# Talking-heads attention and a sparse-activation feed-forward on one core: a weight conversion two slots later, operand splits in other steps, two gates in another form

## The chip, the cores and the metric

The kernel runs on one core of a Trainium2 chip. The metric is the device time of one execution in microseconds (us); the median of three executions of the kernel before is 889.9 us (888.41 to 891.25).

The engines are called as in the profile: PE is TensorE's matmul and PEld its weight load, DVE is VectorE, ACT is ScalarE, POOL is GpSimd, and SP is the engine whose queue issues nearly all DMAs here. Each engine works through its own instructions in the order in which the program gives them and waits at an instruction until its semaphores allow it.

## What is computed

The reference, cut to what matters (batch 4, 12 heads, 448 rows, head size 64; then 1792 tokens, 768 wide, 2048 inner):

```python
scores = scale * np.matmul(q, k.transpose(0, 1, 3, 2))
scores = np.einsum('bhij,hg->bgij', scores, w_pre)
attn = np.exp(scores - scores.max(-1, keepdims=True))
attn = attn / (attn.sum(-1, keepdims=True) + 1e-9)
attn = np.einsum('bhij,hg->bgij', attn, w_post)
x = (attn @ v).transpose(0, 2, 1, 3).reshape(B * S, H * D)
h = x @ w_in
g = np.where(h >= 1, h, np.where(h <= -1, 0.0, (h + 1) ** 2 / 4))
out = g @ w_out
```

The two weights of the second half, w_in and w_out, come as float64, and the kernel turns them into float32 by integer work on their words.

## The kernel before

**Attention stage (to about 460 us).** The 16 tiles of 120 or 88 query rows are cut into blocks of ten rows times twelve heads; three groups of three or four blocks make a tile, so there are 48 groups, and the main loop (`for n in range(NG + 2)`) runs one group a turn, 8 to 11 us each. In a turn, every engine's order is: `load_s` of the next group (SP), `pre` (PE, the first head mix), `row_max` (DVE, L205), one `split` (DVE, L189 and L190), `exps` (ACT, L211), `norm` (DVE L217 and L218, then POOL L222), further splits, a first call of `convs`, `post` of the group before (PE L232, evicted by ACT L234), transposes, `pv` (PE L249), `scores` (PE L157, evicted by ACT L162 and DVE L166), late loads, and a second call of `convs`. One `post` of the group before stands among the exponentials. `pre`, `post`, `pv` and the scores share six PSUM buffers (`ps_l`), which `exps` and the evictions give back.

**The conversion.** `conv_units` has 64 chunks of 128 x 384 float64 values. Each goes through a load (SP L327, into `wraw`, three buffers), `scaled` (ACT L288), `lowest` (ACT L294), `shifted` (DVE L297), `sign` (DVE L303, the last reader of `wraw`), `add` (POOL L307) and a store (SP L334). The work is dealt out in slots: chunk n is loaded in slot 3n, and each later step follows at the lag that the table `lags` gives it. `convs(goal)` runs slots until their number reaches a goal; the goals are `share * (n - NC + 0.4)` in the middle of a group and `share * (n - NC + 1)` at its end, with `share` = slots / 41. There are 203 slots before. So most groups run two slots in the middle and three at the end, and which chunk's steps fall into which of the five places goes round every three groups. As 203 / 41 is 4.95, the pattern slips by one slot at group 22.

**First feed-forward product (about 461 to 679 us).** It is a seven-product scheme, in 56 steps `j`: `q, k = divmod(j, 7)`, with the first 28 steps over 2 x 512 tokens (phase 0) and the other 28 over 2 x 384 (phase 1). `step(j)` is 18 matmuls at L510 with the operand `xop[ph, k]` (named a0 to a6 and b0 to b6 in the profile). After it, a turn gives ACT and DVE in this order: `split_w(j + 2)` (ACT L399, DVE L402), `take_maxima` (DVE L555), a gate, `split_xb` (three times ACT L457 and DVE L458: one operand of phase 1), and `evict_f(j)`. `evict_f` is two copies on ACT (L570) for k = 0, 2 and 3, an addition on DVE (L572) for k = 1, 4 and 5. The products of k = 0, 2, 4 and 6 share one bank, so `step` of k = 6 has to wait for the eviction of k = 4. A `gate` in the short form is one ACT instruction (L538) and two on DVE (L549 and L550); in the long form it is three on ACT (L538, L545, L546) and one on DVE a step later (L555). After `split_xb(k)`, `load_xb` on SP fetches the pieces of the operand four places on.

**Second product (679 us to the end).** PE at L675 works without a break.

Of the kernel before, what the change touches and what calls it, by code (L numbers as in the profile page):

```python
# [22 lines left out]
def tile_talking_heads_moe(  # L23
# [248 lines left out]
    def convert(st, p):  # L272

        def halves():  # L280
            w = st["raw"].bitcast(I32).rearrange("p (n t) -> p n t", t=2)
            return w[:, :, 0], w[:, :, 1]

        def scaled():
            lo, hi = halves()
            if "t" not in st:
                st["t"] = p.tile([128, CW], I32, tag="wt", name="wt", bufs=4)
            nc.scalar.activation(out=st["t"].bitcast(F32), in_=hi.bitcast(F32), func=AF.Copy,  # L288
                                 scale=2.0 ** -111)

        def lowest():
            lo, hi = halves()
            st["k"] = p.tile([128, CW], I32, tag="wk", name="wk", bufs=2)
            nc.scalar.activation(out=st["k"], in_=lo.bitcast(U32), func=AF.Copy, scale=2.0 ** -29)  # L294

        def shifted():
            nc.vector.tensor_single_scalar(out=st["t"], in_=st["t"], scalar=3,  # L297
                                           op=ALU.logical_shift_left)

        def sign():  # L300
            lo, hi = halves()
            t = st["t"]
            nc.vector.scalar_tensor_tensor(out=t, in0=hi, scalar=-0x80000000, in1=t,  # L303
                                           op0=ALU.bitwise_and, op1=ALU.bitwise_or)

        def add():
            nc.gpsimd.tensor_tensor(out=st["t"], in0=st["t"], in1=st.pop("k"), op=ALU.add)  # L307

        return [scaled, lowest, shifted, sign, add]

    def conv_units():
        chunks = []
        for f in range(NF):
            for c in range(2):
                chunks.append((w_in[c * CW:(c + 1) * CW, f * 128:(f + 1) * 128]
                               .rearrange("(k p) f -> p k f", p=128), wsd[f, c]))
            for c in range(2):
                chunks.append((w_out[f * 128:(f + 1) * 128, c * CW:(c + 1) * CW],
                               wod[f, :, c * CW:(c + 1) * CW]))
        st = {}  # L320
        us = []

        def load(n):
            raw = qp.tile([128, CW], I64, tag="wraw", name="wraw", bufs=3)
            src = chunks[n][0]
            dst = raw if len(src.shape) == 2 else raw.rearrange("p (k f) -> p k f", f=128)
            nc.sync.dma_start(out=dst, in_=src)  # L327
            st[n] = {"raw": raw}
            st[n]["steps"] = convert(st[n], qp)

        def store(n):
            dst = chunks[n][1]
            src = st.pop(n)["t"].bitcast(F32)
            nc.sync.dma_start(out=dst, in_=src)  # L334


        lags = ((store, 11), (4, 6), (2, 4), (3, 4), (1, 3), (0, 2), (load, 0))
        for slot in range(3 * len(chunks) + 11):
            def unit(slot=slot):
                for f, lag in lags:  # L340
                    n, rest = divmod(slot - lag, 3)
                    if rest == 0 and 0 <= n < len(chunks):
                        if callable(f):
                            f(n)
                        else:
                            st[n]["steps"][f]()
            us.append(unit)
        return us
# [6 lines left out]
    NQ = NF // 4  # L355
# [71 lines left out]
    def split_w(j):  # L427
        if j < NJ:
            wts[j] = split_to(raw[KIND[j % 7], j // 7] if j < NJA else raw.pop(j))
# [22 lines left out]
    def split_x(x, r, k, ph):  # L452
        p, off = HOMES[ph][k]
        n = NH[ph]
        hi, lo = xop[ph, k, r] = [view(f"{'ab'[ph]}{k}{'hl'[i]}", p, off + 8 * n * r + 4 * n * i, n, dt=F32R)
                                     for i in range(2)]
        nc.scalar.activation(out=hi, in_=x, func=AF.Copy)  # L457
        nc.vector.tensor_tensor(out=lo, in0=x, in1=hi.bitcast(F32), op=ALU.subtract)  # L458
# [13 lines left out]
    def x_last(r):  # L472
        sum_x("B21", "B21", "B22", r)
# [18 lines left out]
    def load_xb(p):  # L492
        if p < 21:
            k, r = divmod(p, 3)
            piece[p] = view("xr", *RING[p % 12], NH[1])
            nc.sync.dma_start(out=piece[p], in_=x_src(XK[k], r, 1) if k in (0, 1, 5) else xtd[XK[k], r])

    def split_xb(k):
        for r in range(3):
            split_x(piece.pop(3 * k + r), r, k, 1)  # L500
        for r in range(3):
            load_xb(3 * k + r + 12)
# [22 lines left out]
    def slot(q, i, h):  # L525
        ph = q // NQ
        return gq[ph, q % NQ].rearrange("p (n i) t -> p n i t", i=2)[:, :, i, h * NH[ph]:(h + 1) * NH[ph]]
# [29 lines left out]
    def gate_slot(q, i, h, act=False):  # L557
        d = slot(q, i, h)
        gate(bk.pop(q) if (i, h) == (1, 0) else d, d, act)
# [161 lines left out]
    with tc.manual_schedule():  # L721
# [194 lines left out]
        for z in range(NQ):  # L916
            gq[0, z] = view("gq", "gg", 16384 * z, 4, NA)
            gq[1, z] = view("gq", *GHOME[z], 4, 2 * NH[1])
        XAT = {23: 0, 24: 1, 25: 2, 26: 3, 27: 4, 29: 5, 30: 6}
        for j in range(NJ):  # L920
            q, k = divmod(j, 7)
            ph = j // NJA
            end = q == NQ - 1
            if j:
                step(j)
                split_w(j + 2)
                take_maxima()
            else:
                evict_f(0)
            if k == 0 and q:  # L930
                gate_slot(q - 1, 1, 0)
            elif k == 1 and q:
                if ph == 0:
                    sum_w("A21", "A22", "A11", ALU.subtract, q)
                gate_slot(q - 1, 0, 1)
            elif k == 3:
                gate_slot(q, 0, 0, q > 0)
            elif k == 4 and q:
                gate_slot(q - 1, 1, 1, True)
            if j == 0:  # L940
                sum_w("S1", "A21", "A22", ALU.add, 0)
                sx("B12", 2, 4)()
                sx("B11", 2, 3)()
                x_last(2)
                for r, s in enumerate(("s4", "s2", "s6")):
                    load_xa("B22", r, s)
            elif j == 1:
                sum_w("A21", "A22", "A11", ALU.subtract, q)
            elif j == 2:
                for r in range(3):  # L950
                    split_xa("B22", r, 5)
            elif j == 3:
                for r in range(3):
                    split_xa("B21", r, 6)
            if ph == 0:
                if k == 0:
                    keep_w(2, q)
                    keep_w(3, q)
                elif k == 2:
                    sum_w("A12", "A12", "A11", ALU.subtract, q)  # L960
                    keep_w(4, q)
                    load_b(NJA) if end else load_a("A11", q + 1)
                elif k == 3:
                    keep_w(5, q)
                    load_b(NJA + 1) if end else load_a("A21", q + 1)
                elif k == 4:
                    if end:
                        load_b(NJA + 2)
                        load_b(NJA + 3)
                    else:  # L970
                        load_a("A22", q + 1)
                        load_a("A12", q + 1)
                elif k == 5 and not end:
                    sum_w("S1", "A21", "A22", ALU.add, q + 1)
                elif k == 6 and not end:
                    sum_w("A11", "S1", "A11", ALU.subtract, q + 1)
            load_b(j + 6) if j + 2 >= NJA else None
            if 4 <= j < 7:
                tx_load(j - 4)
            if 6 <= j < 18:  # L980
                tx_sum(j - 6)
            if 7 <= j < 19:
                tx_keep(j - 7)
            if 19 <= j < 22:
                for p in range(4):
                    load_xb(4 * (j - 19) + p)
            if j in XAT:
                split_xb(XAT[j])
            if j:
                evict_f(j)  # L990
            f = j - NJ + 3
            if f == 0:
                load_t(0)
                load_t(1)
            elif f == 1:
                split_t(0)
                load_t(2)
                prep_s(0)
            elif f == 2:
                split_t(1)  # L1000
                load_t(3)
                prep_s(1)
# [62 lines left out]
```

## Time and profile before

| | us |
|---|---|
| three executions: median (lowest to highest) | 889.9 (888.41 to 891.25) |
| the profiled execution: its time | 888.03 |
| the profiled execution: span from first to last instruction | 886.3 |
| PE busy in the span | 867.8 (98%) |
| DVE busy | 680.0 (77%) |
| ACT busy | 566.8 (64%) |
| POOL busy | 178.2 (20%) |

A busy PE in this profile is one with a matmul under way by its modelled end; the end is later than the moment from which the next matmul could be issued. Lines such as "L303" are lines of the kernel before; "SPq" is the instruction by which SP issues a DMA.

### The profile page before, as it was taken

The page shows a single profiled execution, that of the slowest core. Times are in us where ns is not written, and L with a number is a line of the kernel's source. Part 1 is how long each engine was busy: PE and PEld are TensorE (multiplying, and loading weights), DVE is VectorE, ACT ScalarE, POOL GpSimd, SP SyncE. Part 2 cuts the span into 40 slices and gives each one's busy share as a digit, 9 for nine tenths or more (in the row PEclk, how much of TensorE's full clock was granted, in tenths as well). Part 3 has the DMA queues.
Part 4 walks back from the last instruction along what each step waited for, and adds up shares of the span by engine and source line. Part 5 has one row for each costly group of instructions (what it writes and reads, how often), then busy time and mean ns, then how long its engine had stood idle before and what let it go on. Part 6 is the DMA issues. An engine that isn't in the chain of part 4 may idle for free.

```text
span 886.3 us, 17512 instructions
## 1 busy us (share of the span) xinstructions
PE 867.8 (98%) x6410; PEld 763.0 (86%) x6410; DVE 680.0 (77%) x1121; ACT 566.8 (64%) x1157; POOL 178.2 (20%) x253
## 2 busy tenths in 40 slices
PE   8999999999999999999999999999999999999998
PEld 6788888888888878878788788879999999999998
DVE  4887787888687887887568977788667987777853
ACT  4787677776877777877675566677667535433431
POOL 0334433543443533534220000000000000000000
PEclk9999999999999999999999999999999999999999
DMA  8768867888678887786355745654444453124341
GB/s 159 236 185 240 256 200 225 268 236 244 192 238 257 236 253 201 237 258 201 123 183 172 267 153 177 215 173 129 125 126 161 137 184 134 54 65 132 98 134 62
DMA packets 155832, 162.30 MB, mean 183 GB/s; under 512 B 64100, under 2 KB 149476, under 8 KB 155748
## 3 DMA queue, kind: packets, MB, share of 16 engines
q1 hardware_dynamic: 152964, 160.51, 59.6%
q10 hardware_dynamic: 2784, 0.69, 0.5%
q8 instruction: 51, 0.84, 0.4%
q14 instruction: 33, 0.27, 0.1%
HBM read 88.81 MB, written 33.82 MB: 138 GB/s over the span
## 4 chain that ended last, share of the span: by engine, by line
PE 82%; DMA 9%; ACT 4%; DVE 2%; SPq 2%; issue 1%; POOL 0%; ACTq 0%; DVEq 0%
PE ps_f L675 23%; PE ps_f L510 22%; PE ps_a L232 12%; PE ps_x L249 7%; PE ps_l L202 6%; PE ps_s L157 6%; PE ps_l L200 4%; DMA wraw<-in_moe_w_in_dram 3%; DMA s<-ssb 3%; DMA wraw<-in_moe_w_out_dram 2%; ACT e L211 1%; SPq L181 1%; PE ps_t L140 1%; ACT wt L288 1%; DMA qraw<-in_q_dram 1%
## 5 line engine op out<-in xcount | busy, mean ns | idle before, releaser
L222 POOL TENSOR_SCALAR wr<-wpost,rs 120x120 f32<-120x120 f32 x180 | 114.0, 649 | 264.1 <-DVE rs L218 212.7
L232 PEld LDWEIGHTS ps_a<-wr,e 120*112 120x112 f32 x1440 | 155.0, 177 | 12.8 <-issue 10.7
L232 PE MATMUL ps_a<-wr,e 120*112 120x120 f32 (+1 forms) x1440 | 157.0, 266 | 4.9 <-ACT e L211 4.9
L211 ACT ACTIVATE e<-ps_l,nm 120x448 f32<-120x448 f32 x180 | 112.5, 632 | 43.6 <-DVE nm L205 43.3
L658 ACT ACTIVATE sgh_p<-gq_p 128x1024 fp32r<-128x1024 f32 (+1 forms) x56 | 53.3, 953 | 90.8 <-PE ps_f L675 90.6
L205 DVE TENSOR_REDUCE nm<-ps_l 120x1 f32<-120x448 f32 x180 | 100.9, 615 | 6.1 <-PE ps_l L202 5.5
L402 DVE SCALAR_TENSOR_TENSOR wl<-wi,wh 128x768 fp32r<-128x768 f32 x71 | 67.6, 954 | 43.9 <-ACT wh L399 43.9
L675 PE MATMUL ps_f<-wh,sgl_p 128*128 128x384 f32 x294 | 98.2, 334 | 0.0
L675 PE MATMUL ps_f<-wh,sgh_p 128*128 128x384 f32 x294 | 98.2, 334 | 0.0
L675 PE MATMUL ps_f<-wl,sgh_p 128*128 128x384 f32 x294 | 98.2, 334 | 0.0
L234 ACT ACTIVATE aT<-ps_a 112x480 f32<-112x480 f32 x180 | 94.9, 597 | 3.4 <-PE ps_a L232 3.3
L399 ACT ACTIVATE wh<-wi 128x768 fp32r<-128x768 f32 x71 | 59.6, 842 | 58.2 <-PE ps_f L510 17.9
L202 PE MATMUL ps_l<-s,wpre 120*120 120x448 f32 x196 | 94.1, 563 | 0.2 <-DMA s<-ssb 0.2
L659 DVE TENSOR_TENSOR sgl_p<-gq_p,sgh_p 128x1024 fp32r<-128x1024 f32 (+1 forms) x56 | 60.9, 1088 | 35.8 <-ACT sgh_p L658 35.8
L249 PE MATMUL ps_x<-aT,v 112*64 112x120 f32 (+1 forms) x1536 | 83.5, 262 | 1.5 <-ACT aT L234 1.4
L249 PEld LDWEIGHTS ps_x<-aT,v 112*64 112x64 f32 x1536 | 73.8, 137 | 7.6 <-ACT aT L234 2.7
L166 DVE COPY ssb<-ps_s 120x448 f32<-120x448 f32 (+1 forms) x96 | 57.3, 619 | 17.2 <-PE ps_s L157 17.1
L307 POOL TENSOR_TENSOR wt<-wt,wk 128x384 int32<-128x384 int32 x64 | 64.2, 1010 | 20.6 <-ACT wk L294 15.2
L162 ACT ACTIVATE ssb<-ps_s 120x448 f32<-120x448 f32 (+1 forms) x96 | 51.9, 548 | 17.3 <-PE ps_s L157 14.3
L200 PE MATMUL ps_l<-sh,wpre_h 120*120 120x448 f32 (+1 forms) x82 | 58.6, 715 | 0.0
L190 DVE TENSOR_TENSOR sl<-s,sh 120x448 fp32r<-120x448 f32 (+1 forms) x82 | 54.2, 662 | 2.8
L675 PEld LDWEIGHTS ps_f<-wh,sgh_p 128*128 128x128 f32 x294 | 55.2, 188 | 0.0
(210 smaller groups left out, 1837.0 us busy)
## 6 DMA issues: line engine op xcount, KB each, us to landing
s<-ssb SPq DMA_DIRECT2D x172, 210.0 KB
wraw<-in_moe_w_in_dram SPq DMA_DIRECT2D x32, 384.0 KB
wraw<-in_moe_w_out_dram SPq DMA_DIRECT2D x32, 384.0 KB
wi<-wod SPq DMA_DIRECT2D x29, 384.0 KB
wi<-wsd SPq DMA_DIRECT2D x28, 384.0 KB
wsd<-wt SPq DMA_DIRECT2D x32, 192.0 KB
wod<-wt SPq DMA_DIRECT2D x32, 192.0 KB
wi<-wss SPq DMA_DIRECT2D x16, 384.0 KB
```

The lines of the kernel that those rows point to most:

```text
L200: nc.tensor.matmul(out=lps[m], lhsT=w[:k], rhs=y[:k], start=(j == 0), stop=(j == 2))
L202: nc.tensor.matmul(out=lps[m], lhsT=wpre[:k], rhs=x[:k], start=True, stop=True)
L205: nc.vector.tensor_reduce(out=nm, in_=lps[m], axis=AX.X, op=ALU.max, negate=True)
L211: nc.scalar.activation(out=e, in_=ps, func=AF.Exp, bias=nm, accum_out=sm[:, j:j + 1])
L222: nc.gpsimd.tensor_scalar_mul(out=w[:, :, :ni], in0=wpost[:, :, :ni], scalar1=rs[:, j:j + 1])
L232: nc.tensor.matmul(out=ps[:, r, :ni * H], lhsT=e[:, r * KP:(r + 1) * KP], rhs=w[:, :, :ni], start=True, stop=True)
L234: nc.scalar.activation(out=aT[t][:, :, :, c:c + ni], in_=ps[:, :, :ni * H].rearrange("q r (h i) -> q r h i", h=H), func=AF.Copy)
L249: nc.tensor.matmul(out=ps[s * D:(s + 1) * D, m, :n], lhsT=vt[b, g][:, 2 * m + s, r * D:(r + 1) * D], rhs=a[:, r, 4 * g + 2 * m + s, :n], s ...
L307: nc.gpsimd.tensor_tensor(out=st["t"], in0=st["t"], in1=st.pop("k"), op=ALU.add)
L402: nc.vector.scalar_tensor_tensor(out=lo, in0=t, scalar=2.0 ** -8, in1=hi.bitcast(F32), op0=ALU.mult, op1=ALU.subtract)
L510: nc.tensor.matmul(out=o, lhsT=u[:, c, k], rhs=x, start=first and r == 0 and m == 0, stop=r == 2 and m == 2, skip_group_check=True)
L675: nc.tensor.matmul(out=o, lhsT=x[:, f, c], rhs=y[:, f % 2, :], start=first and f == 0 and m == 0, stop=hf == 1 and f == 3 and m == 2, skip ...
```

## The change

All steps of a conversion but its load come two slots later (their distances to one another stay), which makes 205 slots out of 203. The phase 1 operands are split in the steps 23, 23, 26, 27, 27, 30 and 31 in place of 23, 24, 25, 26, 27, 29 and 30. The gates at k = 3 of q = 3 and q = 4 (steps 24 and 31) take the short form, as the one of q = 0 does.

```diff
-        lags = ((store, 11), (4, 6), (2, 4), (3, 4), (1, 3), (0, 2), (load, 0))
-        for slot in range(3 * len(chunks) + 11):
+        lags = ((store, 13), (4, 8), (2, 6), (3, 6), (1, 5), (0, 4), (load, 0))
+        for slot in range(3 * len(chunks) + 13):
...
-        XAT = {23: 0, 24: 1, 25: 2, 26: 3, 27: 4, 29: 5, 30: 6}
+        XAT = {23: (0, 1), 26: (2,), 27: (3, 4), 30: (5,), 31: (6,)}
...
             elif k == 3:
-                gate_slot(q, 0, 0, q > 0)
+                gate_slot(q, 0, 0, q not in (0, NQ - 1, NQ))
...
-            if j in XAT:
-                split_xb(XAT[j])
+            for x in XAT.get(j, ()):
+                split_xb(x)
```

## Rows read from the trace of the kernel before

**Rows 1.** The page, part 1: busy time, share, instructions of each engine.
```profile
PE 867.8 (98%) x6410; PEld 763.0 (86%) x6410; DVE 680.0 (77%) x1121; ACT 566.8 (64%) x1157; POOL 178.2 (20%) x253
```

**Rows 2.** Waits of PE, 0 to 465 us: waiter, releaser, total us, times, longest.
```profile
PE ps_a L232 <- ACT e L211: 4.9, 7, 1.2
...
PE ps_x L249 <- ACT aT L234: 1.4, 3, 0.6
```

**Rows 3.** Waits of ACT, 30 to 440 us, same columns.
```profile
ACT wt L288 <- DMA wraw<-in_moe_w_out_dram: 14.5, 6, 3.4
...
ACT wt L288 <- DMA wraw<-in_moe_w_in_dram: 11.1, 7, 3.1
```

**Rows 4.** Timeline, 391 to 400 us: start, us, engine, line, operation, [idle before].
```profile
392.34 0.87 SPq L327 DMA_DIRECT2D wraw<-in_moe_w_out_dram  x1
...
393.73 0.55 ACT L294 ACTIVATE wk<-wraw 128x384 int32<-128x384 uint32 x1
...
395.84 2.21 DVE L205 TENSOR_REDUCE nm<-ps_l 120x1 f32<-120x448 f32 x4
...
397.70 0.54 ACT L288 ACTIVATE wt<-wraw 128x384 f32<-128x384 f32 x1 [3.42 <-DMA wraw<-in_moe_w_out_dram]
...
399.00 1.25 PE L232 MATMUL ps_a<-wr,e 120*112 120x120 f32 x10 [1.18 <-ACT e L211]
```

**Rows 5.** Timeline, 185 to 194 us, a group in which pv waits.
```profile
185.19 2.08 POOL L307 TENSOR_TENSOR wt<-wt,wk 128x384 int32<-128x384 int32 x2
...
186.46 1.24 DVE L303 SCALAR_TENSOR_TENSOR wt<-wraw,wt 128x384 int32<-128x384 int32 x1
...
192.72 1.45 PE L249 MATMUL ps_x<-aT,v 112*64 112x120 f32 x24 [0.53 <-ACT aT L234]
```

**Rows 6.** Timeline, 577 to 591 us, steps 26 (a5) and 27 (a6).
```profile
577.66 0.39 PE L510 MATMUL ps_f<-a5h_p,wl 128*128 128x512 f32 x1
...
580.04 1.06 ACT L546 ACTIVATE ga_p<-ga_p 128x1024 f32<-128x1024 f32 x1
...
581.54 1.49 DVE L458 TENSOR_TENSOR b2l_p<-xr_p,b2h_p 128x384 fp32r<-128x384 f32 x3 [1.64 <-ACT b2h_p L457]
...
582.96 1.22 DVE L572 TENSOR_TENSOR gq_p<-ps_f,gq_p 128x1024 f32<-128x1024 f32 x1
...
584.23 0.50 PE L510 MATMUL ps_f<-a6h_p,wl 128*128 128x512 f32 x1 [2.20 <-DVE gq_p L572]
...
590.08 0.33 PE L510 MATMUL ps_f<-b0h_p,wl 128*128 128x384 f32 x1
```

**Rows 7.** Windows: us, busy by engine (instructions), PEclk, DMA share, GB/s.
```profile
586.00:587.00 1.00, 1.00 (x4) 0.71 (x4) 1.00 (x3) 0.29 (x1) 0.00 (x0) 0.50 0.73 203
```

**Rows 8.** Timeline of PE, first matmul of step 20 and of step 21.
```profile
553.04 0.39 PE L510 MATMUL ps_f<-a6h_p,wl 128*128 128x512 f32 x1
...
557.25 0.39 PE L510 MATMUL ps_f<-a0h_p,wl 128*128 128x512 f32 x1
```

**Rows 9.** Groups by line: count, busy us, mean ns, idle before.
```profile
L545 ACT ACTIVATE ga_p<-ga_p,cs 128x1024 f32<-128x1024 f32 (+1 forms) x14 | 14.6, 1046 | 0.5
...
L549 DVE SCALAR_TENSOR_TENSOR ga_p<-ga_p 128x1024 f32<-128x1024 f32 (+1 forms) x10 | 10.9, 1086 | 0.2
```

**Rows 10.** Timelines of DVE and of PE: eviction of step 32, start of step 34.
```profile
607.19 0.95 DVE L572 TENSOR_TENSOR gq_p<-ps_f,gq_p 128x768 f32<-128x768 f32 x1
...
608.79 0.34 PE L510 MATMUL ps_f<-b6h_p,wl 128*128 128x384 f32 x1
```

**Rows 11.** Timelines of SP and DVE, 130 to 142 us (group 12).
```profile
132.71 0.37 SPq L327 DMA_DIRECT2D wraw<-in_moe_w_out_dram  x1
...
134.64 0.69 DVE L190 TENSOR_TENSOR sl<-s,sh 120x448 fp32r<-120x448 f32 x1
...
140.73 0.38 DVE L189 CAST sh<-s 120x448 fp32r<-120x448 f32 x1
```

**Rows 12.** The chain that ended last: start, us, what (one of five such pieces).
```profile
384.07 5.79 DMA s<-ssb
```

## The prediction

> **What bounds the kernel now.** The page's first part comes first: PE is busy in 98% of the span, the next engine in 77% [rows 1]. So a change off PE can only give back what PE loses in waits, and the waits of PE are the second view. In the attention stage they are two lines, 4.9 us in 7 waits for the exponentials and 1.4 us in 3 waits for evicted `aT` [rows 2]. The third view is who held ACT up in that stage: it sat 14.5 + 11.1 = 25.6 us in 13 waits for the converted weights' loads [rows 3]. The timeline of one such place shows how the two hang together [rows 4]: SP issues a load of `wraw` at 392.34, late, in the last bunch of a group; ACT comes to `scaled` of that chunk right after L294 at 393.73 and waits 3.42 us, until 397.70; the row maxima were begun at 395.84, so the first exponential could have run from about 396.4 (one of the four in that row takes 0.55), but it stands behind `scaled` on ACT; the PSUM buffers come back late and PE waits 1.18 us before 399.00. The fourth view is the first feed-forward product, where PE has one large wait: 2.20 us before step 27, for the addition L572 that evicts step 25 [rows 6]. After it the granted clock was 0.50, that is 1.2 in place of 2.4 GHz [rows 7].
>
> **A PE wait is a little more than its row says.** Step 26 starts at 577.66, step 27 at 584.23, step 28 at 590.08 [rows 6]. A step of phase 0 with nothing in its way, step 20, takes 557.25 - 553.04 = 4.21 us [rows 8]. The two steps took 12.42 us and should take 8.42: 4.00 us lost, of which 6.57 - 4.21 = 2.36 by the wait and 5.85 - 4.21 = 1.64 by the half clock behind it. The row of the wait says 2.20, so each wait costs some 0.16 more than shown, because the matmul before it is counted to its modelled end. Ten waits in the attention stage are then 6.3 + 1.6 = 7.9 us [rows 2]. That is the most the first part of the change can give.
>
> **Part 1, the conversion two slots later.** No instruction is added or taken away: per chunk one load, two ACT, two DVE, one POOL instruction, one store. Two empty slots more cost nothing. `share` becomes 205 / 41 = 5 exactly, so the pattern of two and three slots no longer slips at group 22.
> What goes: of the five places in a group, a load in the third place (first of the end bunch) had its `scaled` in the fifth, in the same bunch, behind only one more ACT instruction [rows 4]. 3n falls on that place in every fifth chunk, 13 of 64. With lag 4 that `scaled` comes in the middle bunch of the next group, behind the next exponentials. In rows 4 that is at or after 395.84 + 0.55 + four exponentials of about 0.6 us = 398.8, and the data were there at 397.70: 1.1 us to spare. The closest pair that remains is a load in the middle bunch whose `scaled` ends that group; it was two slots, it is four now. All seven waits for exponentials lie in or just behind such groups, so 4.9 + 7 x 0.16 = 6.0 us go; and of the waits for `aT` one lies in such a group too.
> What stays: the other two waits for `aT` have another cause. In rows 5 `sign` takes 1.24 us beside two POOL additions that began at 185.19, so the next maxima and exponentials are late, and two conversion steps stand on ACT ahead of the evictions that PE waits for (0.53 us). That order of steps isn't removed but moves one group on. Two such waits were seen; from nothing to three (one in each later batch, the pattern no longer slipping) may follow, at 0.53 to 0.65 + 0.16 each; I take two, 1.5 us. Attention: 7.9 - 1.5 = 6.4 us, between 4.0 (three, and some waits for loads left at the closest pair) and 7.9.
> The Trainium skill (SBUF — State Buffer, Who interferes with whom) says that a VectorE instruction with two SBUF inputs and a GpSimd instruction that reads SBUF shut each other out of a shared port for a whole instruction. The trace agrees at `sign`, 1.24 us beside the additions [rows 5]. By that rule the collision is bound to come back wherever the moved `sign` meets an addition, in all three batches, and the sum would be about 0.7 us smaller.
> Queues passed: SP's loads keep their slots, but the buffer that a load takes is freed by `sign` of the chunk three before, which was five slots ahead and is now three. Behind a waiting load stand the store and then the next group's four `load_s`, which DVE's splits wait for. In group 12 SP is at such a load at 132.71, while DVE ends its last split at 135.33 and would then do the middle `sign`, about 136.2: SP would stand 3.5 us. The split that needs the next group's rows is at 140.73 [rows 11], some 4.1 us after the shifted issue at 136.6. I price this at nothing, as the split's own queue has time; the bound is in the rivals.
>
> **Part 2, splits and gates.** Taken together, since both empty ACT and DVE ahead of step 27. Before: ACT runs the long gates of steps 24 and 25, ends the second at 581.10 [580.04 + 1.06, rows 6], then splits b2; DVE waits 1.64 us for b2h and only after b2l comes L572 at 582.96, although step 25 had ended at about 577.8. After, with the durations of the trace: b1 is split in step 23, right behind b0 (ACT has idle time there, the eviction has to wait for the step's end). In step 24 the gate is one ACT instruction, and DVE takes its two (1.09 and about 1.1 us by rows 9; 1.2 each at this size), done by about 576.5. In step 25 DVE has `wl` only, to 577.4, and L572 starts when step 25 ends, at about 577.85, done by 579.1. Step 27 may then start at 577.66 + 4.21 = 581.87, with 2.8 us to spare. So the wait of 2.36 us goes, and the half clock with it, 1.64 us: 4.0 us. What the gates cost: on ACT each loses two instructions (L545 and L546, 1.05 and about 1 us), on DVE each gains one (L549, 1.09 us) [rows 9]; PE hides both while DVE keeps ahead of the steps.
> What is late next: I went on through the steps in the same way, all 4.0 us earlier. b2, b3, b4 are split by 583.1, 586.5 and 587.9, and wanted at 592.3, 595.4 and 598.5; b5 and b6 by 597.8 and 601.9, wanted at 601.7 and 604.8. The closest is step 34, which waits for the eviction of step 32. Before, that ended at 607.19 + 0.95 = 608.14 with the step at 608.79, 0.65 us to spare [rows 10]; after, it ends at about 603.7 with the step at 604.8, 1.1 us to spare. SP's part (three loads in step 23 behind the others, those for b6 a step later) has 7 us or more at each place. Part 2 gives 4.0 us, between 2.4 (the wait but not the clock) and 4.0.
>
> **The sum.** 6.4 + 4.0 = 10.4 us. The profiled execution took 888.03 us (span 886.3 and 1.7 around it): 877.6 after. It stands 1.9 us below the median of the executions shown, 889.9; for a median after I take the same step from the median: 889.9 - 10.4 = 879.5 us.
>
> **The rivals.**
> *The attention gain is given back.* ACT no longer waits, but DVE's maxima come as late as in rows 5, through the moved order of steps, so PE waits elsewhere for the exponentials. For it: the two waits already seen without a late load; against it: most groups show no PE wait at all, in all of the orders of steps. At 1 to 3 us of 7.9 kept: 889.9 - 4.0 - 2 = about 884.
> *The stall at step 27 only moves.* The DVE work added by the gates makes an eviction or a `wl` late somewhere in steps 28 to 35, and the clock falls again. For it: spare times of 1 to 2 us there; against it: the closest one is no worse than before. Part 2 gives nothing: 889.9 - 6.4 = 883.5.
> *Slower: SP stands too long.* The load's shorter distance to `sign` holds back `load_s`. Such a transfer takes up to 5.79 us [rows 12]; with 4.1 us between issue and use, DVE waits up to 1.7 us and with it the next exponentials. 27 of the loads follow a `sign` of the same group; about half find SP far enough ahead to wait. 13 x 1.7 = 22 us at full price, 889.9 - 10.4 + 22 = 901.5. It decides from where more than 0.8 us in each of these groups reach PE.
> *It doesn't do what it says.* If the loads, not the place of `scaled`, were the limit (the DMA engines full), each `scaled` would still wait in its new place and PE with it: 889.9 - 4.0 = 886 with part 2, about 889.9 without. Against it: two slots are over 3 us, as much as the longest wait [rows 3].
>
> **How the numbers follow.** Both gains as summed 0.62; attention gain given back 0.15; stall moved 0.10; no effect 0.07; slower 0.06. The likeliest gives 879.5. Its own range is 877.9 (7.9 + 4.0) to 883.5 (4.0 + 2.4). The range that should hold the time 8 times in 10 takes in the two rivals at 884, and about 2 us below for the spread of the executions: 876 to 885.5. A measurement can tell about 0.3%, 2.7 us, from no change: faster than 887.2 are the first three and part of the fourth, 0.90; within 0.3%, 0.05; slower, 0.05.
>
> **What would show it.** In the profile after: ACT's waits for `wraw` at L288 down from 25.6 us to under 4; PE's waits for exponentials gone, at most three for `aT`; no PE wait before a6 and a granted clock of full speed from there on; the order of ACT b0h, b1h before the copies of step 23. Wrong would be: SP standing at L327 for L303 over 20 us with DVE's waits for `s` grown from there, or a new PE wait on L572 in steps 28 to 35.

## The result, and the profile after

The changed kernel takes 880.4 us (median of 6 executions, 877.5 to 882.7), the kernel before 890.8 us in the same comparison: a ratio of 0.988, with a 95% interval from 0.986 to 0.991. That is 10.4 us less; the prediction had 10.4. The sum was right, but in the attention stage that was luck: two of its terms were both too small, by about the same amount, and the section on the steps says which.

The profiled execution of the changed kernel took 880.27 us (span 878.6). The page's line of engines:

```profile
PE 866.5 (99%) x6410; PEld 763.1 (87%) x6410; DVE 682.7 (78%) x1123; ACT 563.1 (64%) x1153; POOL 178.8 (20%) x253
```

PE's work is the same, 6410 instructions; its share rose from 98% [rows 1] to 99%. ACT has 4 instructions fewer and DVE 2 more, the gates of part 2. Against the profiled execution of before, 888.03 us, 7.76 us went: 4.8 in the attention stage (from the first `pre` of group 0 to the first matmul of the product, 437.5 to 432.75), 4.0 in the first product (217.8 to 213.8), while group 0 began 0.8 us later and the rest differs by 0.2.

The waits of PE from 0 to 465 us in the changed kernel (waiter, releaser, us in total, times, longest):

```profile
PE ps_x L249 <- ACT aT L234: 1.2, 2, 0.6
PE ps_a L232 <- ACT e L211: 1.0, 2, 0.7
```

The waits for exponentials fell from 4.9 us in 7 to 1.0 in 2, those for `aT` from 3 to 2 [rows 2]. The waits of ACT, 30 to 440 us, one line of before and then those after:

```profile
ACT e L211 <- DVE nm L205: 38.3, 35, 2.2
```

```profile
ACT e L211 <- DVE nm L205: 50.3, 44, 2.3
...
ACT wt L288 <- DMA wod<-wt: 1.8, 2, 1.0
ACT wt L288 <- DMA wsd<-wt: 1.3, 3, 0.9
```

No wait for `wraw` is left of the 25.6 us in [rows 3]. In its place `scaled` (L288) waits 3.1 us for something that the prediction had not named: the store of the chunk that used the same `wt` buffer. About half of what ACT no longer spends on raw data it spends waiting for maxima (`e` for `nm`, 38.3 us before and 50.3 now), while PE's own waits for the exponentials fell. SP and DVE in the same stretch, first before, then after:

```profile
SPq L327 <- DVE wt L303: 6.0, 5, 2.7
...
DVE sh L189 <- DMA s<-ssb: 18.1, 18, 1.7
```

```profile
SPq L327 <- DVE wt L303: 36.8, 23, 8.0
...
DVE sh L189 <- DMA s<-ssb: 26.4, 22, 2.0
```

This is the sign by which the prediction wanted to be told wrong: SP now stands 36.8 us at the loads for `sign`, and DVE's waits for `s` grew by 8 us. PE hardly noticed. Experiments below ask why.

The first product, steps 25 to 28 (a4, a5, a6, b0) by the first matmul of each, and the instructions of DVE that matter, from one timeline:

```profile
569.68 0.39 PE L510 MATMUL ps_f<-a4h_p,wl 128*128 128x512 f32 x1
...
573.76 0.39 PE L510 MATMUL ps_f<-a5h_p,wl 128*128 128x512 f32 x1
...
573.96 1.22 DVE L572 TENSOR_TENSOR gq_p<-ps_f,gq_p 128x1024 f32<-128x1024 f32 x1 [0.43 <-PE ps_f L510]
...
577.79 1.49 DVE L458 TENSOR_TENSOR b2l_p<-xr_p,b2h_p 128x384 fp32r<-128x384 f32 x3
...
577.96 0.39 PE L510 MATMUL ps_f<-a6h_p,wl 128*128 128x512 f32 x1
...
582.16 0.33 PE L510 MATMUL ps_f<-b0h_p,wl 128*128 128x384 f32 x1
```

The addition L572 that evicts step 25 now waits for PE, not PE for it. It ends at 575.18, 2.8 us ahead of step 27. Steps 25, 26 and 27 take 4.08, 4.20 and 4.20 us; steps 26 and 27 took 6.57 and 5.85 before [rows 6].

For the attention stage one more measure is needed, since the waits shown are not all that PE loses. The 48 groups repeat a pattern of twelve. For each of the twelve places I took the shortest period (first `pre` matmul to the next group's first) seen in the profiles as what the group takes undisturbed; what groups 5 to 41 take above it is called the loss. It depends by 0.3 to 0.5 us on which profiles the shortest periods are taken from. Before it is 8.3 us, after 3.65 us.

### The profile page after: what moved, and what is told of

Its sections match the earlier page's. It is cut to its first block, busy times and chain, and to the rows that moved or that the text cites. A ratio compares the mean times of both kernels' runs of the same rounds, so it can differ in the third digit from the quotient of the medians.

```text
span 878.6 us, 17523 instructions
## 1 busy us (share of the span) xinstructions
PE 866.5 (99%) x6410; PEld 763.1 (87%) x6410; DVE 682.7 (78%) x1123; ACT 563.1 (64%) x1153; POOL 178.8 (20%) x253
## 4 chain that ended last, share of the span: by engine, by line
PE 90%; DVE 3%; ACT 2%; DMA 2%; issue 1%; SPq 1%; ACTq 0%; DVEq 0%
PE ps_f L675 23%; PE ps_f L510 21%; PE ps_a L232 15%; PE ps_x L249 8%; PE ps_l L202 8%; PE ps_s L157 7%; PE ps_l L200 5%; DMA kraw<-in_k_dram 1%; ACT e L211 1%; PE ps_t L140 1%; PE ps_k L123 1%; DMA qraw<-in_q_dram 1%; DVE wt L303 1%; SPq L181 0%; DVE ssb L166 0%
## 5 line engine op out<-in xcount | busy, mean ns | idle before, releaser
L222 POOL TENSOR_SCALAR wr<-wpost,rs 120x120 f32<-120x120 f32 x180 | 114.4, 651 | 259.1 <-DVE rs L218 188.2
L307 POOL TENSOR_TENSOR wt<-wt,wk 128x384 int32<-128x384 int32 x64 | 64.5, 1014 | 21.1 <-ACT wk L294 16.4
L166 DVE COPY ssb<-ps_s 120x448 f32<-120x448 f32 (+1 forms) x96 | 56.8, 618 | 12.3 <-PE ps_s L157 11.9
```

The lines of the kernel that those rows point to most:

```text
L222: nc.gpsimd.tensor_scalar_mul(out=w[:, :, :ni], in0=wpost[:, :, :ni], scalar1=rs[:, j:j + 1])
```

## Experiments

What a run saves is worked out from its ratio, which isn't exactly the ratio of the two medians.

**One part alone.** First the conversion's steps two slots later, the rest as before:

```diff
-        lags = ((store, 11), (4, 6), (2, 4), (3, 4), (1, 3), (0, 2), (load, 0))
-        for slot in range(3 * len(chunks) + 11):
+        lags = ((store, 13), (4, 8), (2, 6), (3, 6), (1, 5), (0, 4), (load, 0))
+        for slot in range(3 * len(chunks) + 13):
```

> Only the conversion two slots later; splits and gates as before. If the two parts of the change act apart from each other, this has the attention stage of the changed kernel (from the first head mix of group 0 to the first matmul of step 0: 432.8 us, against 437.5 before) and the first product of the kernel before (wait of 2.2 us before step 27, then half clock: 4.0 us lost). Time about 890.8 - 5 to 6 = 885 to 886. If instead the gain of the change is all in the product, it is at 890.

Measured: 884.7 us against 889.1, a ratio of 0.995 (0.993 to 0.997), that is 4.4 us. Its profiled execution has an attention stage of 437.6 us and a loss of 8.4, although the program of that stage is the changed kernel's (3.65). So the loss isn't fixed by the program.

Then the splits and the gates alone, the conversion as before:

```diff
-        XAT = {23: 0, 24: 1, 25: 2, 26: 3, 27: 4, 29: 5, 30: 6}
+        XAT = {23: (0, 1), 26: (2,), 27: (3, 4), 30: (5,), 31: (6,)}
...
-                gate_slot(q, 0, 0, q > 0)
+                gate_slot(q, 0, 0, q not in (0, NQ - 1, NQ))
...
-            if j in XAT:
-                split_xb(XAT[j])
+            for x in XAT.get(j, ()):
+                split_xb(x)
```

> Only the splits in other steps and the two short gates; conversion as before. Parts acting apart: attention stage as before (437.5 us), no wait before step 27 and no half clock behind it, 4.0 us less: about 886.8. If the wait only moves, a new PE wait appears in steps 28 to 35 and the time stays at 889 to 891.

Measured: a ratio of 0.9979 (0.9958 to 0.9999), 1.9 us (the medians, 886.5 and 889.1, differ by 2.6). The product took 213.8 us, 4.0 less than before, and there was no wait before step 27; but the attention stage of that execution took 439.8 us, 2.3 more than in the profile of before, with a loss of 10.5.

**Which of the two edits removes the stall.** The splits moved, the gates as before (the first and third hunk above):

> Only the splits in other steps, both gates long. By my working the splits alone are enough: the eviction of step 25 (L572) no longer stands behind b2l and starts behind L555 at about 579.8, done at 581.0, step 27 due at 581.9: no wait, 4.0 us gained. If the gates are needed as well, step 27 still waits 1 us or more, and whether the clock falls behind a wait of that size can be read.

and the gates in the short form, the splits as before (the second hunk):

> Only the two gates in the short form, splits as before. ACT is some 2 us ahead in step 25, b2h is ready at about 579.4 instead of 581.5, L572 runs from about 580.8 to 582.0, step 27 is late by 0.2 us or not at all and the clock stays: 3.8 to 4.0 us gained. If the splits are what counts, the wait stays over 1 us.

Measured: each alone removes it. The product takes 214.5 us with the splits alone and 214.1 with the gates alone, 213.8 with both; in neither is there a wait for L572. So the prediction's "taken together, since both empty ACT and DVE ahead of step 27" was more than was needed: either edit is worth 3.3 to 3.7 of the 4.0 us, in one execution each.

The run with the splits alone took 890.0 us all the same, and its attention stage shows why the old order of steps is costly. The same load's `scaled` in ACT's timeline, in the kernel before and then in this run; PE's waits from 270 to 300 us and one window of this run (us, busy by engine, PEclk, DMA share, GB/s):

```profile
283.41 0.55 ACT L288 ACTIVATE wt<-wraw 128x384 f32<-128x384 f32 x1 [3.07 <-DMA wraw<-in_moe_w_out_dram]
```

```profile
285.26 0.54 ACT L288 ACTIVATE wt<-wraw 128x384 f32<-128x384 f32 x1 [4.99 <-DMA wraw<-in_moe_w_out_dram]
```

```profile
PE ps_a L232 <- ACT e L211: 2.7, 1, 2.7
```

```profile
286.00:288.00 2.00, 1.44 (x7) 1.47 (x8) 0.68 (x2) 2.00 (x8) 0.00 (x0) 0.50 1.09 209
```

With the same program for this stage, the load of this `wraw` held ACT up for 4.99 us in place of 3.07 (the longest such wait before was 3.42 [rows 4]); PE waited 2.7 us, the granted clock was 0.50 (1.2 GHz) afterwards, and this one group lost 6.0 us. How late a load comes, then, differs from one execution to the next.

**Does SP's standing at L327 make `s` late?** The changed kernel with a fourth `wraw` buffer; the space comes from one of the eight `e` buffers:

```diff
-            raw = qp.tile([128, CW], I64, tag="wraw", name="wraw", bufs=3)
+            raw = qp.tile([128, CW], I64, tag="wraw", name="wraw", bufs=4)
...
-        e = ap_.tile([KM, S], F32, tag="e", name="e", bufs=8)
+        e = ap_.tile([KM, S], F32, tag="e", name="e", bufs=7)
```

> The changed kernel with four raw buffers in place of three (room for it from the exponentials, seven buffers in place of eight). The order of every engine's work stays. The changed kernel loses 3.7 us of PE in the attention stage, in groups 7, 13, 16, 28, 31 and 40, all of one place in the round of three. Theory of places: the loss comes from where the conversion's steps stand among the others; SP's wait at the loads for sign (36.8 us in 23 waits) goes to under 10 us, and the PE loss stays between 2.5 and 4.5 us. Theory of the buffer: SP standing at the loads holds back load_s and with it the splits and maxima; then the loss falls under 1.2 us.

Measured: 881.4 us (one execution), as the changed kernel. SP's longest wait and its wait for `sign`, DVE's wait for `s` (all 30 to 440 us), and one place on PE:

```profile
SPq L181 <- DVE ssb L166: 52.1, 13, 10.5
...
SPq L327 <- DVE wt L303: 2.0, 3, 1.0
```

```profile
DVE sh L189 <- DMA s<-ssb: 27.8, 21, 2.6
```

```profile
170.01 1.87 PE L232 MATMUL ps_a<-wr,e 120*112 120x120 f32 x16 [1.25 <-ACT e L211]
```

SP's wait for `sign` fell from 36.8 to 2.0 us. SP stands elsewhere instead, DVE still waits 27.8 us for `s`, and the loss is 6.3 us. So the theory that this wait makes `s` late falls, and with it the reason for the slower rival: the 36.8 us at L327 held back nothing that was urgent.

**Are two slots needed?** One slot later in place of two (`lags` of 12, 7, 5, 5, 4, 3, 0):

> The changed kernel with the conversion one slot later than before in place of two. A load in the third place is still converted in the next group's middle, so the 25.6 us of ACT waits for raw loads should go as well. The pair of ACT steps in the middle of a group, with a sign in the bunch ahead, now falls on the groups whose number leaves 2 by 3, where neither kernel has lost PE time without a late load. Theory of places: PE loses under 1.2 us in the attention stage (before 8.3, changed 3.7): about 878. Theory of the buffer: sign is four slots ahead of the load, halfway, and the loss is about half of the changed kernel's, 1.5 to 2.5 us. Third: lag one leaves waits for loads, loss over 4 us.

Measured: a ratio of 0.991 (0.988 to 0.995), and 16.0 us of waits for `wraw` are left, of 25.6. ACT, 30 to 440 us:

```profile
ACT wt L288 <- DMA wraw<-in_moe_w_in_dram: 8.4, 4, 2.8
ACT wt L288 <- DMA wraw<-in_moe_w_out_dram: 7.6, 6, 3.4
```

One slot removes a third of these waits and two remove all. The time doesn't tell the two apart, as the intervals overlap; I had expected that one slot would do as well in the trace, and it doesn't. Its profiled execution, the slowest of its four, has an attention stage of 439.2 us, no shorter than before (437.5).

**Is the gain the even share of slots?** The kernel before with two empty slots more and nothing else (the range to `3 * len(chunks) + 13`), so that `share` is 5:

> The kernel before with two empty slots at the end of the conversion, so that there are 205 slots and the pattern of two and three doesn't slip at group 22; lags, splits and gates as before. If the later steps are what gains in the attention stage, this gains nothing there: ACT waits for raw loads stay at 20 us or more, PE loses 7 to 10 us (8.3 before). If the end of the slip is what gains, the loss falls to 4 us.

Measured: 886.8 us (one execution), attention loss 9.6 us, 23.3 us of waits for `wraw`. The even share alone doesn't remove the waits or the loss. This run also shows something on the clock: it has the stall before step 27, but what followed differs. PE's wait and the window behind it in this kernel, and then the same two in the conversion alone, timed a second time below:

```profile
PE ps_f L510 <- DVE gq_p L572: 2.2, 1, 2.2
...
586.00:587.00 1.00, 1.00 (x6) 0.78 (x5) 1.00 (x3) 0.60 (x2) 0.00 (x0) 1.00 0.48 126
```

```profile
PE ps_f L510 <- DVE gq_p L572: 2.2, 1, 2.2
...
582.00:583.00 1.00, 1.00 (x3) 0.74 (x3) 1.00 (x3) 0.00 (x0) 0.00 (x0) 0.50 0.91 310
```

The same wait of 2.2 us, behind the same work, is followed by the full clock once and by half of it once. Here the product took 216.3 us, there 217.8.

**The whole and its parts on one chip.** The parts had given 4.4 + 1.9 = 6.3 us, the whole 10.4. To see whether that gap is real, all three ran again beside one another:

> The changed kernel once more, beside its two parts on the same chip. So far the parts gave 0.995 and 0.9979 of the kernel before, 0.993 together, and the whole 0.9884: about 4 us more than the parts. Theory 'the parts add and the difference is the chips' and the executions': here the whole saves what the two runs beside it save together, within 2 us. Theory 'the whole gains more than its parts' (the half clock behind the stall at step 27, or another order of loads): 3 us or more above their sum again. A second profile of the same program also tells how far the attention stage's loss is the program's: 3.65 us in the first profile; the same six groups (7, 13, 16, 28, 31, 40) and 3 to 5 us if it is fixed by the order of steps, up to 8 us in other groups if it is drawn anew in each execution.

> The conversion's steps two slots later, the product as before, beside the whole change. Forecast of the prediction: 6.4 us less than before; the first run gave 4.3. Here 4 to 6.5 us less if the chip made the difference, 4.3 again if not. Its attention stage is the same program as in the whole change: a loss of 3.6 to 8.4 us, in groups one behind a multiple of three above all.

> Splits and gates alone, the conversion as before, beside the whole change. Forecast of the prediction: 4.0 us less, of which 2.4 for the wait and 1.6 for the half clock behind it; the first run gave 1.9 us. Theory 'the half clock comes in most executions of the kernel before': 4 us. Theory 'only in some': 2.4 to 3 us or less.

| Kernel | Median us | Ratio to before (890.1) | Saved us | Attention loss us, profiled execution |
|---|---|---|---|---|
| both parts | 881.0 | 0.990 (0.987 to 0.993) | 9.1 | 5.7 |
| conversion alone | 883.7 | 0.993 (0.991 to 0.995) | 6.3 | 4.4 |
| splits and gates alone | 886.1 | 0.995 (0.993 to 0.998) | 4.1 | 11.8 |

Now the parts give 6.3 + 4.1 = 10.4 us and the whole 9.1, so no gain beyond the parts was there to be explained: the gap of the first runs was scatter, between executions or between chips. The two timings of the conversion alone have intervals that overlap, and so have the two of the product.

**What makes the loss that remains?** Two suspects: `sign` (L303) taking 1.24 us beside POOL's addition, as in [rows 5], and rows of `s` that come late. In the profiled execution of the changed kernel both meet in group 28; its timeline:

```profile
274.22 0.39 DVE L189 CAST sh<-s 120x448 fp32r<-120x448 f32 x1 [1.80 <-DMA s<-ssb]
...
276.32 2.15 POOL L222 TENSOR_SCALAR wr<-wpost,rs 120x120 f32<-120x120 f32 x3
...
276.90 0.56 DVE L303 SCALAR_TENSOR_TENSOR wt<-wraw,wt 128x384 int32<-128x384 int32 x1
...
278.44 2.07 POOL L307 TENSOR_TENSOR wt<-wt,wk 128x384 int32<-128x384 int32 x2
...
279.69 1.25 DVE L303 SCALAR_TENSOR_TENSOR wt<-wraw,wt 128x384 int32<-128x384 int32 x1
...
280.85 2.20 DVE L205 TENSOR_REDUCE nm<-ps_l 120x1 f32<-120x448 f32 x4
...
282.37 0.84 PE L232 MATMUL ps_a<-wr,e 120*112 120x120 f32 x6 [0.73 <-ACT e L211]
```

DVE waits 1.80 us for `s`, later takes 1.25 us for `sign`, and the maxima at 280.85 are so late that PE waits 0.73 us for the exponential behind them. The changed kernel with the addition left out (the low words of the converted weights aren't added, so that part of the computation is missing):

```diff
         def add():
-            nc.gpsimd.tensor_tensor(out=st["t"], in0=st["t"], in1=st.pop("k"), op=ALU.add)
+            st.pop("k")
```

> The changed kernel without POOL's addition of the low words in the conversion and in the splits that use the same steps: that part of the computation is left out. Theory 'sign beside the addition': L303 never takes 1.24 us any more, always about 0.56, the maxima come 0.7 us earlier where they were late, and of the attention stage's loss of 3.65 to 8.4 us under 1.5 stays. Theory 'late s': the waits of DVE for the transfers of s stay at 20 us or more and the loss stays at 3 us or more, with L303 short. In both the product is as in the changed kernel, 213.8 us.

Measured: 881.7 us (one execution). The groups of `sign` and of `s` in DVE's list (count, busy us, mean ns, idle before):

```profile
L303 DVE SCALAR_TENSOR_TENSOR wt<-wraw,wt 128x384 int32<-128x384 int32 x64 | 36.5, 570 | 2.2
L189 DVE CAST sh<-s 120x448 fp32r<-120x448 f32 x75 | 28.4, 378 | 40.0 <-DMA s<-ssb 40.0
```

`sign` takes 0.57 us on average in place of 0.63, and never more than 0.7; the waits for `s` rise to 40.0 us and the loss is 6.9. The theory that `sign` beside the addition makes the loss falls, as under 1.5 us should have stayed. Only group 40, which loses 0.4 to 1.2 us in the five other profiles with this order of steps and rows at their usual time, lost nothing here. The waits for `s` grew by far more than the 4 us that `sign` saved; why the rows came so late in this execution isn't shown.

**The rows earlier.** If late rows were all, issuing them earlier should give the loss back. In the changed kernel the loads of `s` for the second and third group of a tile go out in the middle of the turn before, ahead of the conversion steps of its middle and end bunch:

```diff
-            if n + 1 < NG:
+            if n + 1 < NG and (n == 0 or n % 3 == 2):
                 for m in (*groups[n + 1][1::2], *groups[n + 1][::2]):
                     load_s(m)
...
             for m in nxt:
                 split(m)
+            if n + 2 < NG and n % 3 != 1:
+                for m in (*groups[n + 2][1::2], *groups[n + 2][::2]):
+                    load_s(m)
             convs(share * (n - NC + 0.4))
```

> The changed kernel, with the loads of s for the second and third group of each row tile issued half a group earlier, behind the group's last split and ahead of its end bunch of conversion steps; the loads for the first group of a tile stay, since its scores are not there earlier. Nothing is left out. Theory 'late rows of s': the losses of the changed kernel lie in groups one behind a multiple of three, whose rows were waited for 1.2 to 2.3 us; they are there now 4 us earlier, so DVE's waits for s fall from 26 us to under 12 and the loss of the attention stage from 3.65 to 5.7 us to 2 us or less; the median is 2 to 4 us under that of the changed kernel, a ratio of 0.985 to 0.987. Theory 'steps on ACT and DVE in the way' (the order of the conversion's steps holds back the maxima and the evictions, whenever s comes): the waits for s fall just so, but the loss stays at 3 us or more in the same groups, and the ratio is 0.988 to 0.991 as before. A third way: the rows go out together with the conversion's transfers and the v loads are late in their turn; then DVE or PE waits for these and the ratio is above 0.991.

Measured: 899.2 us against 889.0, a ratio of 1.009 (1.006 to 1.012), so slower than the kernel before and some 18 us behind the changed kernel, and the third way of the expectation in a form that it hadn't named. DVE's waits for `s` fell to 8.3 us (30 to 450 us) as forecast, and groups 28 and 40 lost 0.2 us each where the changed kernel had lost 0.5 to 1.1 in two profiles, although `sign` took 1.24 us there. But ACT now waits for stores, and PE for ACT (waits of DVE and of ACT, 30 to 450 us, and of PE, 0 to 465 us):

```profile
DVE sh L189 <- DMA s<-ssb: 8.3, 9, 2.2
```

```profile
ACT wt L288 <- DMA wsd<-wt: 21.7, 6, 7.0
...
ACT wt L288 <- DMA wod<-wt: 13.0, 6, 4.6
```

```profile
PE ps_a L232 <- ACT e L211: 15.5, 12, 4.8
```

The largest of them, group 15, from the timelines of POOL, SP, ACT and PE and a window:

```profile
149.17 1.00 POOL L307 TENSOR_TENSOR wt<-wt,wk 128x384 int32<-128x384 int32 x1
...
150.66 6.89 SPq L181 DMA_DIRECT2D s<-ssb  x8
...
158.20 0.45 SPq L334 DMA_DIRECT2D wsd<-wt  x1
...
166.00 0.55 ACT L288 ACTIVATE wt<-wraw 128x384 f32<-128x384 f32 x1 [6.98 <-DMA wsd<-wt]
...
167.30 0.91 PE L232 MATMUL ps_a<-wr,e 120*112 120x120 f32 x3 [4.75 <-ACT e L211]
```

```profile
160.00:170.00 10.00, 5.25 (x33) 4.88 (x32) 5.34 (x12) 4.00 (x12) 1.04 (x2) 0.83 1.00 261
```

The chunk is ready for its store at 150.17. SP then issues eight loads of `s` in a row, for two groups, of which the changed kernel has only the first four ahead of this store, and comes to the store at 158.20; with the DMA engines full (share 1.00) the store lands just before 166.0. Until then its `wt` buffer isn't free, `scaled` waits 6.98 us on ACT, the exponentials stand behind it, and PE waits 4.75 us; the clock is down in part of this window (0.83). The attention stage takes 454.4 us in place of 432.8 to 434.8.

## Why the prediction was right, step by step

**A wait is a little more than its row says.** Held in the product: it became 4.0 us shorter in each profile with both edits (213.8 us, eight of eight), and in the padded kernel, where the clock stayed up, a wait shown as 2.20 cost 2.5 us. In the attention stage the rule gives a little too little: 7.9 us where the loss is 8.3, and for the four waits after 2.8 where it is 3.65.

**Part 2, the stall at step 27.** Right to a tenth. Step 27 came 2.8 us after L572's end, as forecast. Counted from step 27, the splits of b2, b3 and b4 ended 1.3, 4.7 and 6.1 us behind its start (forecast 1.2, 4.6 and 6.0), and step 34 came 1.2 us after the eviction of step 32 (forecast 1.1):

```profile
598.75 0.95 DVE L572 TENSOR_TENSOR gq_p<-ps_f,gq_p 128x768 f32<-128x768 f32 x1
...
600.88 0.34 PE L510 MATMUL ps_f<-b6h_p,wl 128*128 128x384 f32 x1
```

One thing was taken as certain that isn't: the half clock behind the wait, 1.64 us of the 4.0. It followed in three of the four profiles with the stall (before, and the conversion alone twice), not in the padded one. So the part is worth about 2.4 or 4.0 us by the execution; the prediction had both as ends of its range, and took 4.0. And each edit alone would have been worth most of it. (By its own terms the lower end of the forecast's own range is 889.9 - 11.9 = 878.0, not 877.9.)

**Part 1, what goes.** The mechanism was right: a `scaled` too close behind its load. No wait for `wraw` was left, and most waits for exponentials went; two stayed where none was forecast. The size of the term was read from one execution, and that was a mild one. Programs with the old order of steps show losses of 8.3 (before), 10.5, 11.8, 12.2 and 14.2 us in five profiles, 11.4 on average. The cap of 7.9 us, called the most that this part can give, was the cap of that execution only. There was a sign of it: that execution stands 1.9 us below the median, as the prediction says in its sum.

**Part 1, what stays.** The step that failed: 1.5 us for two waits for `aT` behind a slow `sign`, moved one group on. Four profiles of the new order show losses of 3.65, 4.4, 5.7 and 8.4 us, 5.5 on average. They did move by one group: most lie in groups one behind a multiple of three (7, 13, 16, 28, 31, 40). But `sign` isn't their cause by itself, as the run without the addition showed; with rows that came early, two of those groups lost next to nothing although `sign` was slow, so late rows are part of the cause there. Groups 7 and 31 lost some 0.6 to 1.2 us in every profile with the steps two slots later, each with a wait for `aT` of 0.5 to 0.7 us. Group 7 in the changed kernel, from the timeline:

```profile
84.07 0.56 DVE L303 SCALAR_TENSOR_TENSOR wt<-wraw,wt 128x384 int32<-128x384 int32 x1
...
88.10 0.58 ACT L288 ACTIVATE wt<-wraw 128x384 f32<-128x384 f32 x1
...
88.55 0.58 ACT L294 ACTIVATE wk<-wraw 128x384 int32<-128x384 uint32 x1
...
89.02 1.51 ACT L234 ACTIVATE aT<-ps_a 112x480 f32<-112x480 f32 x3
...
89.65 1.55 PE L249 MATMUL ps_x<-aT,v 112*64 112x120 f32 x26 [0.64 <-ACT aT L234]
```

`sign` isn't slow here, and in no profile is it slow in group 7 or 31; nor was it in group 6 of the kernel before, where the other of the two waits in question lay (at 78.30 us). What does stand there each time are two conversion steps on ACT, 0.92 us together, ahead of the evictions that PE waits for. So the prediction read rows 5 half rightly: the order of steps came back one group on, but the slow `sign` belongs to other groups. This is read from the timelines and wasn't tested by moving the pair. With one slot in place of two only one of the steps stands there, and no wait for `aT` above 0.2 us is left, though group 7 loses 1.0 us there too. What makes the rows later in one execution than in another stays open.
The two errors cancel, which is luck: 11.4 - 5.5 = 5.9 us where the prediction had 7.9 - 1.5 = 6.4, and the timed runs of this part gave 4.4 and 6.3.

**Queues passed.** Priced at nothing, rightly, but its bound and its test were wrong. SP stood 36.8 us at L327, above the 20 us that were to refute the prediction, and DVE's waits for `s` rose to 26.4 us; with a fourth buffer the first fell to 2.0 us and the second stayed. SP's wait was slack, and as a test I should have named PE's loss, not SP's standing. By the rule of the Trainium skill (SBUF — State Buffer, Who interferes with whom) that was weighed, the sum would have been 0.7 us smaller. The collision did come back, six times at 1.23 to 1.25 us in the profile of the changed kernel, but taking it away didn't lower the loss (6.9 us).

**The rivals.** The gain given back: in part, 5.5 us stay, but of a larger loss. The stall only moved: no. No effect: no. Slower through SP's order: not here; the run with early rows shows another way in which it can happen. It isn't the reader of the rows that then pays, as the rival had it, but the store behind them in the queue, and with it the buffer that ACT wants.

## What to carry to other kernels

A consumer that sits in an engine's queue ahead of critical work must be given its distance from its load in the worst execution, not the one profiled: read a stage's loss from several executions before you cap a gain with it. A queue that stands at a semaphore isn't yet a cost; ask which engine would have used what is behind it, and look there. Before you issue loads earlier, count the stores that then go out later, and who waits for their buffers.

## What had not been expected of the hardware

The granted clock after a wait of PE isn't settled by the wait: 2.20 us before step 27 was followed by 0.50 in three profiles and by 1.00 in one, and a wait of 2.7 us in the attention stage by 0.50 as well.

When `sign` meets a POOL instruction, it isn't always `sign` that pays. Beside the addition L307 it takes 1.25 us in the timeline of group 28 above (at 279.69). At 276.90 it takes 0.56 us, as alone, although L222 runs beside it. But the L222 that begins before this `sign` ends takes 0.69 us, and the next, beside DVE instructions that read PSUM, 0.58. In the run without the addition a `sign` that begins just behind an L222 takes 0.68 us:

```profile
277.22 0.69 POOL L222 TENSOR_SCALAR wr<-wpost,rs 120x120 f32<-120x120 f32 x1
...
277.89 0.58 POOL L222 TENSOR_SCALAR wr<-wpost,rs 120x120 f32<-120x120 f32 x1
```

```profile
213.30 0.68 DVE L303 SCALAR_TENSOR_TENSOR wt<-wraw,wt 128x384 int32<-128x384 int32 x1
```

Both POOL instructions read SBUF, and by the rule of the Trainium skill that was cited above both contend with `sign`; the trace agrees, but where `sign` alone meets L222 it is some 0.1 us, on one side or the other, and beside the addition 0.7 us on `sign`.

The attention stage of one and the same program differs by nearly 5 us between executions (432.75 and 437.6 us with the new order of steps). The product repeats to within 0.1 us: 213.8 us in all eight profiles with both edits, 217.8 in the three with the stall and the half clock. What in the attention stage differs beyond the lateness of loads and rows isn't shown.
